# A fused attention-and-MLP kernel: other costs and one more dependency in the projections' planner, and two sums of forms on VectorE

## The chip, the cores and the metric

The kernel runs on one core of one Trainium2 chip. The metric is the device time of one execution in microseconds (us), as the median of several executions. Engine names in the profile: PE is TensorE's matmuls, PEld its weight loads, DVE is VectorE, ACT is ScalarE, POOL is GpSimd, SP is SyncE, which issues DMAs.

## The reference

```
x  = A_x;  xn = layernorm(x)                         # 2048 tokens, 640 channels, fp32
q, k, v = split(xn @ wqkv)                           # 32 heads of 20
pq, pk = q @ w_phi, k @ w_phi                        # per head
phi = concat(softmax(p), softmax(-p))                # of pq and of pk
kv, z = phi_k^T v, sum(phi_k);  o = phi_q kv / (phi_q z + 1e-6)
mlp = gelu(layernorm(xn) @ w1 + b1) @ w2 + b2        # 640 -> 1728 -> 640
out = x + o @ wo + mlp
```

## The kernel before, in words

Every fp32 factor is split into two float32r parts, hi and lo, and a product is three matmuls: hi·hi, hi·lo, lo·hi (`mm3`, L69, L70, L71). A tile's hi part is written by ScalarE as a copy, its lo part by VectorE or GpSimd as a subtraction. PE's order is fixed by the program's text, and so is that of the other three engines from the first stage to the end of the projections. The 2048 tokens are four blocks b of 512, or sixteen tiles t of 128.

**First MLP stage, to about 212 us.** `passes(g, b)` multiplies block b with group g of w1, applies the GELU, and adds the product with w2 to an accumulator; blocks 0 and 1 are done here, with other work put between PE's products by a count of ticks. `next_y` makes block 1's normalized input y[1] channel chunk by chunk: GpSimd centres (L694), VectorE scales (L696), ScalarE copies the hi part (L698), VectorE subtracts the lo part (L700). `turned_forms` (L881 to L900) prepares, for blocks 1 and 0, sums and differences of token halves for a product with seven instead of eight block products ("forms"): two sums hi + lo (L886), four differences (L890), ScalarE's hi copies (L894), two lo parts (L896), and stores to DRAM (`f_dram`).

**Projections, about 212 to 429 us.** Tiles t = 0 to 15 are multiplied with the folded weights wkv for q, k and v (L989, or L1360 and L1364 for pairs of tiles 2 to 7, which use the forms). Each result lies in one of three PSUM banks until ScalarE (L1262, L1001, L1083) and VectorE (L1260, L1088) have read it. `feature_steps` then makes softmax features of k and q: extremes (VectorE, L1011 and L1012), differences (GpSimd, L1021), exponentials (ScalarE, L1024), totals (VectorE, L1029), reciprocals (L1035, L1037), products (GpSimd, L1042 for k, L1044 and L1046 for q), and for k a hi copy (ScalarE, L1051) and a lo part (L1054, on GpSimd or VectorE, whichever the planner takes); for q a transposition (L1063). `kv_tile` (L1102, L1105) multiplies a tile's k features with its v, and L1112 adds part of that up.

The order in this stage comes from `Plan` (L1144 to L1212). Each piece of work is added with an engine, a cost in us and the pieces it comes after. `latest` computes for each piece when it must end at the latest for PE's pieces to run without a wait; `run` then places pieces engine by engine, the most urgent among those that can start, on a clock of these costs. Costs of all engines but PE are multiplied by LONGER (L1214). Pieces of SP count another 4.0 us (LANDS) until their data is there. `plan_sums` (L1426) splits the sums of weight forms into hi (L1438) and lo (L1439). When the four splits of the second half are done, `next_forms(0)` (L1463) issues the load of the first turned forms on SP (`load_forms`, L1141): it goes into the place that held these sums. `plan_pair_splits` (L1500) splits the first w1 weights of the next stage, two halves: hi by ScalarE (L1509), lo by GpSimd (L1510); it returns the two lo pieces as `w1_done`. `plan_second_split` does the first half of w2 (L1521, L1525). At the plan's end stand two PE pieces of 3.4 us that emit nothing (L1559): they stand for the next stage's first products, and came after the release of their PSUM banks alone.

**Second MLP stage, from 429 us,** for blocks 2 and 3, with the attention's last steps beside it; the output projection ends the kernel. Its first products are L69 to L71 with the w1 split by L1509 and L1510: fifteen products of the first half, fifteen of the second; after those thirty the last `kv_tile` (t = 15) is put in (`last_kv`), and then come block 3's thirty and the products with w2, which need block 2's hidden values: gelu (L293), hi (L60), lo (L63).

## Time and profile before

| | |
|---|---|
| median of 3 executions | 708.94 us (707.58 to 709.35) |
| the profiled execution | 707.14 us, with a span of 705.4 us |
| mean granted PE clock | 0.998 |
| PE busy | 693.2 us (98%) |
| VectorE, ScalarE, GpSimd busy | 538.1, 373.2, 503.2 us |

The span runs from the first to the last instruction; 1.7 us of the profiled execution's time lie outside of it. A row of a timeline has the start in us from the span's beginning, the duration, the engine, the line, the operation, what is written <- what is read, and in brackets how long the engine was idle before and what released it. PE's matmuls overlap: two of 512 columns start 0.23 us apart, though each is shown as 0.39 us long.

### The profile page before, as it was taken

To read this page: it belongs to the slowest core of one execution; us is meant where nothing else is said; L and a number is where in the kernel's file an instruction comes from. 1 tells how busy PE (TensorE), PEld (TensorE's weight loads), DVE (VectorE), ACT (ScalarE), POOL (GpSimd) and SP (SyncE) were. 2 spreads that over 40 slices of the span, in tenths; PEclk is the share of its full clock that TensorE was granted. 3 is DMA by queue.
4 is the path that set the end of the run, shared out by engine and by line. 5 is a ranking of instruction groups with operands and counts; after the bars stand their busy time and mean duration, and the time that the engine had idled before them with its cause. 6 is when DMAs were issued, how large, how long until landed. Compare 5 with 4: busy or idle time off the path is not lost.

```text
span 705.4 us, 9865 instructions
## 1 busy us (share of the span) xinstructions
PE 693.2 (98%) x3313; PEld 582.8 (83%) x3313; DVE 538.1 (76%) x884; ACT 373.2 (53%) x633; POOL 503.2 (71%) x373
## 2 busy tenths in 40 slices
PE   9999999999999899999999997999999999999998
PEld 7878888888888788888888886888888888888886
DVE  7888664987767988888678868758678687789783
ACT  6435654444444544545455546547677666659360
POOL 3744783767276769898988889648689997477930
PEclk9999999999999999999999999999999999999999
DMA  9816768575531115464631637774345648881212
GB/s 327 257 48 181 238 178 262 180 259 181 185 120 74 60 61 208 106 198 168 151 110 57 148 114 285 199 228 127 123 133 169 182 148 278 294 280 65 76 74 105
DMA packets 72376, 117.06 MB, mean 166 GB/s; under 512 B 8054, under 2 KB 36502, under 8 KB 70318
## 3 DMA queue, kind: packets, MB, share of 16 engines
q1 hardware_dynamic: 72022, 116.42, 51.3%
q8 instruction: 26, 0.43, 0.3%
q14 instruction: 24, 0.20, 0.1%
q10 hardware_dynamic: 304, 0.01, 0.0%
HBM read 76.62 MB, written 39.79 MB: 165 GB/s over the span
## 4 chain that ended last, share of the span: by engine, by line
PE 88%; DVE 6%; POOL 2%; issue 1%; DMA 1%; ACT 1%; DVEq 0%; SPq 0%; ACTq 0%; POOLq 0%
PE bank L989 19%; PE bank L69 18%; PE bank L71 18%; PE bank L70 18%; PE bank L1360 4%; PE bank L1102 2%; PE bank L650 2%; PE bank L1713 1%; PE bank L1714 1%; POOL m L1021 1%; PE bank L1364 1%; PE bank L556 1%; DVE xb L696 1%; DVE y L700 1%; DMA w<-f 1%
## 5 line engine op out<-in xcount | busy, mean ns | idle before, releaser
L69 PE MATMUL bank<-m,w 128*128 128x512 f32 x288 | 113.0, 392 | 0.0
L70 PE MATMUL bank<-m,w 128*128 128x512 f32 x288 | 112.1, 389 | 0.0
L71 PE MATMUL bank<-m,w 128*128 128x512 f32 x266 | 103.6, 389 | 0.0
L989 PE MATMUL bank<-wkh,y 128*128 128x512 f32 (+1 forms) x360 | 101.0, 355 | 0.0
L70 PE MATMUL bank<-y,w 128*128 128x512 f32 (+1 forms) x256 | 99.4, 388 | 0.8 <-DVE y L700 0.8
L69 PE MATMUL bank<-y,w 128*128 128x512 f32 (+1 forms) x256 | 100.2, 391 | 0.0
L71 PE MATMUL bank<-y,w 128*128 128x512 f32 (+1 forms) x246 | 96.0, 390 | 3.8 <-POOL w L1510 3.8
L63 POOL TENSOR_TENSOR w<-r,w 128x640 fp32r<-128x640 f32 x29 | 48.2, 1676 | 34.9 <-ACT w L60 30.3
L989 PEld LDWEIGHTS bank<-wkh,y 128*128 128x128 f32 x360 | 65.0, 188 | 8.1
L69 PEld LDWEIGHTS bank<-m,w 128*128 128x128 f32 x288 | 54.1, 188 | 11.6 <-DVE acc L338 0.4
L989 PE MATMUL bank<-wkl,y 128*128 128x512 f32 (+1 forms) x180 | 63.7, 354 | 0.0
L70 PEld LDWEIGHTS bank<-m,w 128*128 128x128 f32 x288 | 54.1, 188 | 10.9
L71 PEld LDWEIGHTS bank<-m,w 128*128 128x128 f32 x266 | 49.9, 188 | 10.5
L71 PEld LDWEIGHTS bank<-y,w 128*128 128x128 f32 x246 | 46.6, 189 | 14.1 <-POOL w L1510 4.7
L989 PE MATMUL bank<-w,y 128*128 128x512 f32 x240 | 57.5, 391 | 0.0
L70 PEld LDWEIGHTS bank<-y,w 128*128 128x128 f32 x256 | 48.5, 189 | 10.9 <-DVE y L700 1.3
L69 PEld LDWEIGHTS bank<-y,w 128*128 128x128 f32 x256 | 48.5, 190 | 10.4 <-ACT bank L1781 0.3
L338 DVE TENSOR_TENSOR acc<-bank,acc 128x512 f32<-128x512 f32 x70 | 47.2, 683 | 12.6 <-PE bank L71 6.9
L1029 DVE TENSOR_REDUCE sm<-m 128x64 f32<-128x1280 f32 x32 | 47.1, 1471 | 9.0 <-ACT m L1024 8.6
L1262 ACT ACTIVATE m<-bank 128x512 f32<-128x512 f32 (+2 forms) x48 | 20.8, 468 | 58.7 <-PE bank L989 41.1
L989 PEld LDWEIGHTS bank<-w,y 128*128 128x128 f32 x240 | 44.4, 188 | 8.6
L1707 POOL TENSOR_TENSOR e<-e,m 128x512 fp32r<-128x512 f32 x28 | 40.1, 1435 | 15.7 <-ACT m L1706 14.8
(290 smaller groups left out, 1720.5 us busy)
## 6 DMA issues: line engine op xcount, KB each, us to landing
r<-in_w SPq DMA_DIRECT2D x52, 320.0 KB
e<-e SPq DMA_DIRECT2D x40, 256.0 KB
e<-acc SPq DMA_DIRECT2D x52, 160.0 KB
f<-xq SPq DMA_DIRECT2D x16, 256.0 KB
t<-t SPq DMA_DIRECT2D x8, 512.0 KB
acc<-in_xT SPq DMA_DIRECT2D x3, 1280.0 KB
w<-f SPq DMA_DIRECT2D x3, 1024.0 KB
tf<-t SPq DMA_DIRECT2D x2, 1536.0 KB
```

Of the source, the lines that this page charges most:

```text
L63: eng.tensor_tensor(lo, src, f(hi), op=ALU.subtract)
L69: nc.tensor.matmul(ps, lh, rh, start=first, stop=False, **kw)
L70: nc.tensor.matmul(ps, lh, rl, start=False, stop=False, **kw)
L71: nc.tensor.matmul(ps, ll, rh, start=False, stop=last, **kw)
L338: nc.vector.tensor_tensor(acc[b][:, m, :], pw, acc[b][:, m, :], op=ALU.add)
L650: nc.tensor.matmul(ps[:, u * nh * DF:(u + 1) * nh * DF], raw[:nh * DH, u * P:(u + 1) * P], wpt[:nh * DH, g, :nh, 1:], start=True, stop=True)
L989: nc.tensor.matmul(ps, lh[:, kc, c], rh[:, kc], start=n == 0, stop=n == 3 * KC - 1)
L1029: nc.vector.tensor_reduce(sm, e.rearrange("p a (h f) -> p (a h) f", f=DH), axis=AX, op=ALU.add)
L1102: nc.tensor.matmul(kvp[g // 2][:, (g % 2) * 240:(g % 2) * 240 + 240].rearrange("p (i c) -> p i c", i=2), v[:, g * VS:(g + 1) * VS], ft[:, ...
L1262: nc.scalar.activation(o, src, AF.Copy)
L1360: nc.tensor.matmul(ps, left(yn, pl, q), right(w, pr, q), start=first and q == 0 and n == 0, stop=False, skip_group_check=True)
L1707: mlp.after(1, lambda: nc.gpsimd.tensor_tensor(pl, e, f(ph), op=ALU.subtract))
```

## The change

Four edits. The first two sums of `turned_forms` (for block 1, q = 1) go from GpSimd to VectorE. LONGER goes from 1.05 to 1.02, so every cost that is not PE's counts less. The cost of `next_forms(0)` on SP goes from 0.7 to 3.5 us. The two PE pieces at the plan's end also come after `w1_done`.

```
-                nc.gpsimd.tensor_tensor(o, *(f(z[:, c]) for z in y[b]), op=ALU.add)
+                (nc.vector if b and q else nc.gpsimd).tensor_tensor(o, *(f(z[:, c]) for z in y[b]), op=ALU.add)
...
-    LANDS, SOON, HURRY, AFTER, LONGER = 4.0, 0.9, -1.0, 10.0, 1.05
+    LANDS, SOON, HURRY, AFTER, LONGER = 4.0, 0.9, -1.0, 10.0, 1.02
...
-        w_ready["s1"] = (*w_ready["s1"], plan.add("SP", 0.7, lambda: next_forms(0), *done))
+        w_ready["s1"] = (*w_ready["s1"], plan.add("SP", 3.5, lambda: next_forms(0), *done))
...
-        plan.add("PE", 3.4, lambda: None, *bank_free[(n + i) % 3])
+        plan.add("PE", 3.4, lambda: None, *bank_free[(n + i) % 3], *w1_done)
```

PE's order is the same in both kernels. Three places on the other engines:

**The two sums, in the first MLP stage.** On VectorE before (`m_640`, `m_668`: lo parts of hidden values; `wkl`: lo parts of folded weights):

```order
L741 TENSOR_TENSOR wkl<-bank_548,wkh 128x4x6x19
L63 TENSOR_TENSOR m_640<-bank_641,m_640 128x512
L741 TENSOR_TENSOR wkl<-bank_564,wkh 128x6x19
L741 TENSOR_TENSOR wkl<-bank_564,wkh 128x3x6x19
L63 TENSOR_TENSOR m_668<-bank_669,m_668 128x512
```

and now:

```order
L741 TENSOR_TENSOR wkl<-bank_548,wkh 128x4x6x19
L63 TENSOR_TENSOR m_640<-bank_641,m_640 128x512
L886 TENSOR_TENSOR xq<-y_150,y_151 128x512
L741 TENSOR_TENSOR wkl<-bank_564,wkh 128x6x19
L741 TENSOR_TENSOR wkl<-bank_564,wkh 128x3x6x19
L886 TENSOR_TENSOR xq<-y_150,y_151 128x512
L63 TENSOR_TENSOR m_668<-bank_669,m_668 128x512
```

Each sum now stands between two pieces that read PSUM banks. On GpSimd the two stood right behind the five L694, ahead of the four L890; they are gone from there.

**The load of the turned forms, at the start of the projections.** On VectorE before (L1439: lo parts of the weight sums, `w_2148` the place they come from; L1088: reads of PSUM banks for v; the load follows the L1439 of `s`):

```order
L1011 TENSOR_REDUCE mx<-m_2136 128x32
L1012 TENSOR_REDUCE mx<-m_2136 128x32
L1088 SCALAR_TENSOR_TENSOR v_2129<-bank_2240,rs_all,v_2129 128x10x48
L1088 SCALAR_TENSOR_TENSOR v_2129<-bank_2240,rs_all,v_2129 128x32
L1035 RECIPROCAL w<-sm 128x64
L1439 TENSOR_TENSOR acc_2261<-w_2148,acc_2261 128x512
L1439 TENSOR_TENSOR wkl<-w_2148,wkh 128x512
L1439 TENSOR_TENSOR acc_2261<-w_2148,acc_2261 128x512
L1011 TENSOR_REDUCE mx<-m_2135 128x32
L1012 TENSOR_REDUCE mx<-m_2135 128x32
L1088 SCALAR_TENSOR_TENSOR v_2132<-bank_2297,rs_all,v_2132 128x11x12
L1439 TENSOR_TENSOR s_2262<-w_2148,acc_2261 128x512
```

and now:

```order
L1011 TENSOR_REDUCE mx<-m_2136 128x32
L1012 TENSOR_REDUCE mx<-m_2136 128x32
L1439 TENSOR_TENSOR wkl<-w_2148,wkh 128x512
L1088 SCALAR_TENSOR_TENSOR v_2129<-bank_2241,rs_all,v_2129 128x10x48
L1088 SCALAR_TENSOR_TENSOR v_2129<-bank_2241,rs_all,v_2129 128x32
L1439 TENSOR_TENSOR acc_2261<-w_2148,acc_2261 128x512 x2
L1439 TENSOR_TENSOR s_2262<-w_2148,acc_2261 128x512
L1035 RECIPROCAL w<-sm 128x64
L1011 TENSOR_REDUCE mx<-m_2135 128x32
L1012 TENSOR_REDUCE mx<-m_2135 128x32
L1088 SCALAR_TENSOR_TENSOR v_2132<-bank_2297,rs_all,v_2132 128x11x12
```

All four L1439 stand ahead of the reciprocal, of the second pair of extremes and of one L1088; the load needs the last of them.

**The next stage's weights, at the end of the projections.** On GpSimd before, from the first w1 split on (`w_4063`, in the new kernel `w_3934`: the two halves of w1; `w_4183` and `w_4107`: w2; `m_...`: features):

```order
L1510 TENSOR_TENSOR w_4063<-r_4055,w_4063 128x640
L1042 TENSOR_TENSOR m_4069<-m_4069,w 128x1280
L1021 TENSOR_TENSOR m_4151<-m_2136,mx 128x32x20
L1021 TENSOR_TENSOR m_4151<-mx,m_2136 128x32x20
L1510 TENSOR_TENSOR w_4063<-r_4056,w_4063 128x640
L1630 MEMSET kvs 128x1408
```

and now, from the second w1 split on:

```order
L1510 TENSOR_TENSOR w_3934<-r_3910,w_3934 128x640
L1042 TENSOR_TENSOR m_3993<-m_3993,w 128x1280
L1021 TENSOR_TENSOR m_4080<-m_2135,mx 128x32x20
L1021 TENSOR_TENSOR m_4080<-mx,m_2135 128x32x20
L1021 TENSOR_TENSOR m_4104<-m_2136,mx 128x32x20
L1021 TENSOR_TENSOR m_4104<-mx,m_2136 128x32x20
L1525 TENSOR_TENSOR w_4107<-r_4047,w_4107 128x640
L1042 TENSOR_TENSOR m_4080<-m_4080,w 128x1280
L1021 TENSOR_TENSOR m_4159<-m_2136,mx 128x32x20
L1021 TENSOR_TENSOR m_4159<-mx,m_2136 128x32x20
L63 TENSOR_TENSOR w_4107<-r_4048,w_4107 128x640
L1630 MEMSET kvs 128x1408
```

The second L1510 now stands ahead of the last two L1042 and the last three pairs of L1021, and both w2 splits (L1525, L63) ahead of the memset, where they stood behind it and four short products. ScalarE's L1509 and SP's loads move forward with them. Elsewhere in the projections, three of the sixteen lo parts of k (L1054) go from GpSimd to VectorE: ten of VectorE's instead of seven. On VectorE, behind the last `kv_tile`, the lo part of block 2's first hidden values (L63) now stands behind L1112, a reciprocal, five L1619, L1621, the other half's L63 and four L1063; before, it stood ahead of them.

## The prediction

> **What bounds the kernel now.** I read the page first, then the list of PE's waits, then the timelines around each of them.

> ```profile
> PE 693.2 (98%) x3313; PEld 582.8 (83%) x3313; DVE 538.1 (76%) x884; ACT 373.2 (53%) x633; POOL 503.2 (71%) x373
> ...
> PE bank L71 <- POOL w L1510: 3.8, 1, 3.8
> PE bank L1360 <- DMA w<-f: 2.2, 1, 2.2
> ...
> PE bank L70 <- DVE y L700: 0.8, 1, 0.8
> ```

> PE is busy for 693.2 of 705.4 us. PE's work is the same in both kernels, so the change can only act on PE's waits. Besides one at the program's start three are above 0.2 us (columns: sum, times, longest), and they are what the edits aim at: the second half of w1 (L1510), the turned forms' load, and y[1]'s lo part (L700). The first costs more than its 3.8 us. The windows around it (last columns: granted clock, DMA share, GB/s):

> ```profile
> 240.00:244.00 4.00, 1.82 (x8) 1.24 (x7) 4.00 (x5) 1.14 (x1) 2.50 (x2) 1.00 0.62 242
> 245.00:429.00 184.00, 184.00 (x967) 160.26 (x965) 148.49 (x243) 93.43 (x144) 160.91 (x111) 1.00 0.44 129
> ...
> 433.00:437.00 4.00, 0.43 (x2) 0.00 (x1) 3.66 (x5) 1.75 (x3) 4.00 (x3) 1.00 1.01 409
> 437.00:441.00 4.00, 3.74 (x10) 2.99 (x11) 2.96 (x5) 2.56 (x3) 3.84 (x6) 0.57 0.97 402
> ```

> Behind the 3.8 us the clock falls to 0.57 for a few us; behind the 2.2 us (240:244) it stays at 1.00. And from 245 to 429 us PE has no gap at all: 184.00 of 184.00.

> **The change part by part.** First the two sums. PE, VectorE and GpSimd around 41 to 45 us, and what follows the sums:

> ```profile
> 43.77 0.39 PE L69 MATMUL bank<-y,w 128*128 128x512 f32 x1
> 44.99 0.50 PE L70 MATMUL bank<-y,w 128*128 128x512 f32 x1 [0.84 <-DVE y L700]
> 43.10 1.28 POOL L886 TENSOR_TENSOR xq<-y,y 128x512 f32<-128x512 f32 x1 [1.23 <-DVE y L700]
> 44.34 3.63 POOL L890 TENSOR_TENSOR xq<-xq 128x256 f32<-128x256 f32 x4
> 41.02 1.40 DVE L696 TENSOR_TENSOR xb<-xb,m 128x512 f32<-128x512 f32 x1
> 42.34 0.68 DVE L700 TENSOR_TENSOR y<-xb,y 128x512 fp32r<-128x512 f32 x1
> 43.55 1.39 DVE L700 TENSOR_TENSOR y<-xb,y 128x512 fp32r<-128x512 f32 x1
> 57.32 0.69 DVE L63 TENSOR_TENSOR m<-bank,m 128x512 fp32r<-128x512 f32 x1 [1.37 <-ACT m L60]
> 59.24 1.16 ACT L894 ACTIVATE xq<-xq 128x512 fp32r<-128x512 f32 x2
> 63.95 1.37 ACT L60 ACTIVATE w<-r 128x640 fp32r<-128x640 f32 x2 [3.54 <-PE bank L71]
> ```

> VectorE's subtraction takes 0.68 us alone (42.34). While GpSimd runs its second sum (43.10), the last L700 takes 1.39; the L696 ahead of it, beside the first sum, took 1.40: the two engines hold each other up. Without the sums L700 ends 0.72 + 0.71 = 1.4 us earlier, at 43.5 instead of 44.9. PE wants it 0.23 us behind 43.77, at 44.0, so the whole delay of 44.99 - 44.00 = **1.0 us** goes (0.5 if only the later collision matters). The sums cost VectorE 2 x 0.68 around 55 us, where 1.37 us of idle time cover them. GpSimd's four L890 (3.63 us) now start after the sums and end near 60 us, instead of 48; ScalarE wants them at 59.24, and has 3.54 us to spare behind. So I cost the move at nothing; without that cover it would be about 1 us.

> [...]

> Second, the forms' load, with PE's wait, the load (a row of the chain: issue, us to landing) and VectorE's queue:

> ```profile
> 240.91 0.39 PE L1364 MATMUL bank<-wkh,y 128*128 128x512 f32 x1
> 243.48 0.70 PE L1360 MATMUL bank<-m,w 128*128 128x512 f32 x2 [2.18 <-DMA w<-f]
> 238.57 4.77 DMA w<-f
> 229.10 0.81 DVE L1012 TENSOR_REDUCE mx<-m 128x32 f32<-128x640 f32 x1
> 231.07 1.34 DVE L1439 TENSOR_TENSOR acc<-w,acc 128x512 fp32r<-128x512 f32 x1
> 232.34 2.85 DVE L1439 TENSOR_TENSOR wkl<-w,wkh 128x512 fp32r<-128x512 f32 x1
> 235.11 0.68 DVE L1439 TENSOR_TENSOR acc<-w,acc 128x512 fp32r<-128x512 f32 x1
> 237.43 0.99 DVE L1439 TENSOR_TENSOR s<-w,acc 128x512 fp32r<-128x512 f32 x1
> 241.99 0.68 DVE L1260 TENSOR_TENSOR m<-bank,m 128x512 f32<-128x512 f32 x1
> 250.41 1.29 PE L1102 MATMUL bank<-w,v 128*128 128x240 f32 x10
> ```

> PE starts 2.57 us after the matmul before instead of 0.23: 2.34 us lost. In the new order L1439 begins when L1012 ends, near 229.8, with only the two reads of L1088 between (under 0.9). Four at 0.68 make the load start at 233.4; the four measured (1.34 + 2.85 + 0.68 + 0.99 = 5.9) make it 236.6. I take 234.5, nearer the first, because one of the four (235.11) does take 0.68 and GpSimd's product that could hold the others up, L1042, now waits for a reciprocal behind them. Landing 4.77 us later: 239.3, at worst 241.4. PE wants it at 241.1, so the wait is gone, or 0.3. Late next is L1260, which ended at 242.7 and frees a bank that PE now wants 2.3 us sooner; I put 0.3 us on that (0 to 1.3), so **2.0 us** is gained (1.0 to 2.3). The reciprocal and L1042 slip by about the four splits, 3 to 6 us; the features they lead to are wanted by PE only at 250.4 (the first `kv_tile`), which hides it; uncovered it would be those 3 us.

> Third, the next stage's weights:

> ```profile
> 429.08 0.44 PE L69 MATMUL bank<-y,w 128*128 128x512 f32 x1
> 433.04 0.39 PE L70 MATMUL bank<-y,w 128*128 128x512 f32 x1
> 437.26 0.80 PE L71 MATMUL bank<-y,w 128*128 128x512 f32 x1 [3.83 <-POOL w L1510]
> 440.75 0.39 PE L70 MATMUL bank<-y,w 128*128 128x512 f32 x1
> 434.42 2.79 POOL L1510 TENSOR_TENSOR w<-r,w 128x640 fp32r<-128x640 f32 x1
> 429.62 2.38 POOL L1042 TENSOR_TENSOR m<-m,w 128x1280 f32<-128x1280 f32 x1
> 433.19 1.28 POOL L1021 TENSOR_TENSOR m<-mx,m 128x640 f32<-128x640 f32 x1
> 443.49 1.58 POOL L1525 TENSOR_TENSOR w<-r,w 128x640 fp32r<-128x640 f32 x1 [1.50 <-ACT w L1521]
> 433.34 2.47 DVE L1054 TENSOR_TENSOR w<-m,w 128x1280 fp32r<-128x1280 f32 x1 [0.77 <-ACT w L1051]
> 439.64 0.89 DVE L63 TENSOR_TENSOR m<-m,m 128x512 fp32r<-128x512 f32 x1 [1.01 <-ACT m L60]
> 441.66 1.27 DVE L1063 STREAM_TRANSPOSE acc<-m 128x320 f32<-128x320 f32 x3
> ```

> The delay is 437.26 - 433.04 - 0.23 = 3.99 us; then eight matmuls to 440.75 take 3.49 instead of 8 x 0.23 = 1.82 us at the lowered clock: 1.67 more, **5.66 us** in all. The second L1510 now stands ahead of two L1042, six L1021 and L1525, which by these rows take 2 x 2.38 + 6 x 1.28 + 1.58 = 14.0 us. It ends near 437.2 - 14.0 = 423, ten us before PE wants it. This wait goes for sure, and the low clock with it.

> What is late next? (a) Tile 15's `kv_tile` comes after thirty products, 429.1 + 6.9 = 436.0; its lo part (L1054) ended at 435.8. On GpSimd one L1510 and L1525 more now stand ahead of its L1042: 0 to 1.5 us. (b) After sixty products and the `kv_tile`, at about 429.1 + 13.8 + 1.4 = 444.3, PE wants the lo part of the first hidden values, which was ready at 439.64 + 0.89 = 440.5. Now it follows the `kv_tile` (1.29 long, so its end is about 437.3) by fourteen VectorE pieces, itself the last: four L1063 (1.27 / 3 = 0.42 each) and the eight small ones (L1112, L1037, five L1619, L1621) at as much make 5.0, the two L63 between 0.69 (57.32) and 1.39 each (L700's, held up). So it ends between 443.6 and 445.0, and if the small ones take half as long again, at 447.5. I take 1.5 us for (b) (0 to 3), the middle, since L63 can't begin before ScalarE's copy either, and 0.5 for (a) and whatever else crowds there. Both leave the clock alone, since 2.18 us did. Gain: 5.66 - 2.0 = **3.7 us** (1.2 to 5.7).

> LONGER itself makes no work; its trace in the order is three L1054 that move to VectorE. PE's 184.00 of 184.00 covers that, with seven of them there already.

> Sum: 1.0 + 2.0 + 3.7 = **6.7 us**. Against the profiled execution's own 707.14 us (1.7 outside the span, unchanged) this is 700.4; that execution was 1.8 us below the median of 708.94, so I forecast 702.2 us as a median.

> **The rivals.** (1) *The wait only moves.* If the hidden values of (b) come over 3 us late, the clock falls again, since 3.83 us did that, and the third part gives nothing: 1.0 + 2.0 = 3.0 us, 705.9. For: the L63 stands behind pieces that themselves wait for GpSimd. Against: it needs 3 us over the walk above. [...]

> (2) *The order does not do what it says.* ScalarE's L1509 stands earlier in ScalarE's queue; if its raw weights have not landed, it holds all bank reads behind it. If their load takes as long as that of the forms and is issued only as its turn comes, one hold of 4.77 us eats most of the sum: 702.2 + 4.77 = 707.0, which can't be told from no change. Against: the loads move forward together with their users.

> (3) *VectorE becomes the bound: slower.* VectorE's L1054 and GpSimd's work hold each other, and two of the moved ones now stand ahead of an L1088 that frees a bank:

> ```profile
> 239.80 1.47 DVE L1054 TENSOR_TENSOR w<-m,w 128x1280 fp32r<-128x1280 f32 x1
> ```

> If each of the ten makes PE wait, the change turns slower from 0.67 us each (6.7 / 10); at the hold of 2.47 (the L1054 of 433.34) - 1.47 = 1.00 us it is 702.2 + 10.0 = 712.2. Against: the seven of before left PE no gap between 245 and 429 us.

> **How the numbers follow.** The forecast 0.70, (1) 0.14, (2) 0.10, (3) 0.06. The best case is 1.0 + 2.3 + 5.7 = 9.0 us, 699.9; the least of the forecast's is 0.5 + 1.0 + 1.2 = 2.7 us, 706.2, which takes in (1). The three executions of before lie up to 1.4 us from their median; with half of that or so at either end the range is 699.0 to 706.8. About 0.3% (2.1 us) is what a measurement of this kernel can tell from no change: forecast and (1) are faster by more, 0.84; (2) is the same, 0.10; (3) slower, 0.06.

> **What would show it.** In the changed kernel's profile PE's waits for L1510, for w<-f and for L700 are gone; the load is issued near 234 us; the clock stays at 1.00 from 433 to 441 us; a wait of L70 for DVE m L63 appears near 440 us. PE gaps between 245 and 425 us, or a wait over 3 us behind the first sixty products, would make the prediction wrong.

## The result, and the profile after

| | before | changed | ratio, 95% interval |
|---|---|---|---|
| first set, medians of 5 | 709.03 us | 700.23 us | 0.9871 (0.9855 to 0.9888) |
| second set, medians of 23 and 4 | 708.89 us | 699.31 us | 0.9868 (0.9852 to 0.9884) |
| profiled execution shown | 707.14 us | 699.09 us | |

The change makes the kernel 1.3% faster, 9.4 us by the second ratio; forecast were 6.7 us, and the measured time lies in the range, 0.3 to 1.2 us above its lower end of 699.0. In one execution of the first set the granted clock fell to 0.16 at 244 us and stayed there (2847 us; the ratio leaves it out, the median of 5 has it). The profile shown is of the second set (e1 below), with a span of 697.2 us.

The page's engine row, and the list of PE's waits, as they answer to those of before:

```profile
PE 690.6 (99%) x3313; PEld 581.8 (83%) x3313; DVE 540.1 (77%) x889; ACT 372.5 (53%) x633; POOL 491.8 (71%) x368
```

```profile
PE bank L70 <- DVE m L63: 0.8, 1, 0.8
...
PE bank L69 <- DVE v L1088: 0.4, 1, 0.4
```

The waits for L1510, w<-f and L700 are gone. What is new is what the prediction called (b), L70 waiting for the hidden values' lo part, and 0.4 us for a bank. The windows of the same stages (last columns: granted clock, DMA share, GB/s):

```profile
240.00:244.00 4.00, 4.00 (x19) 3.32 (x18) 3.61 (x6) 2.00 (x2) 2.92 (x3) 1.00 0.00 0
245.00:425.00 180.00, 180.00 (x949) 156.96 (x947) 151.90 (x241) 91.59 (x143) 155.56 (x110) 1.00 0.45 135
425.00:429.00 4.00, 3.61 (x18) 2.92 (x17) 4.00 (x8) 2.30 (x5) 3.14 (x3) 1.00 1.01 368
...
433.00:437.00 4.00, 4.00 (x24) 3.47 (x23) 3.16 (x7) 3.99 (x9) 3.84 (x6) 1.00 0.98 408
437.00:441.00 4.00, 4.00 (x19) 3.08 (x17) 4.00 (x10) 1.58 (x4) 3.23 (x3) 1.00 0.60 205
441.00:445.00 4.00, 3.24 (x15) 2.58 (x15) 4.00 (x8) 2.98 (x6) 3.17 (x5) 1.00 0.60 162
```

PE is full from 245 to 425 us, as it was before, although VectorE is busier there (151.90 of 180, where it was 148.49 of 184). The clock stays at 1.00 throughout. The three places in the timelines, first the sums (VectorE, GpSimd, ScalarE):

```profile
43.07 0.68 DVE L700 TENSOR_TENSOR y<-xb,y 128x512 fp32r<-128x512 f32 x1
53.44 0.68 DVE L886 TENSOR_TENSOR xq<-y,y 128x512 f32<-128x512 f32 x1
55.05 0.68 DVE L886 TENSOR_TENSOR xq<-y,y 128x512 f32<-128x512 f32 x1
54.20 0.75 POOL L890 TENSOR_TENSOR xq<-xq 128x256 f32<-128x256 f32 x1 [16.41 <-DVE xq L886]
55.88 2.35 POOL L890 TENSOR_TENSOR xq<-xq 128x256 f32<-128x256 f32 x3 [0.93 <-DVE xq L886]
58.17 1.16 ACT L894 ACTIVATE xq<-xq 128x512 fp32r<-128x512 f32 x2
62.86 1.37 ACT L60 ACTIVATE w<-r 128x640 fp32r<-128x640 f32 x2 [3.54 <-PE bank L71]
```

The last L700 takes 0.68 us again. The sums cost VectorE 0.68 each; GpSimd's differences end at 58.2 us, where ScalarE takes them up, and ScalarE's 3.54 us to spare are untouched. Then the load (VectorE, SP's queue, and PE's first product with the forms):

```profile
228.15 0.81 DVE L1012 TENSOR_REDUCE mx<-m 128x32 f32<-128x640 f32 x1
228.88 1.35 DVE L1439 TENSOR_TENSOR wkl<-w,wkh 128x512 fp32r<-128x512 f32 x1
...
232.44 0.68 DVE L1439 TENSOR_TENSOR s<-w,acc 128x512 fp32r<-128x512 f32 x1
233.27 0.32 SPq L1141 DMA_DIRECT2D w<-f  x1
239.71 0.84 PE L1360 MATMUL bank<-m,w 128*128 128x512 f32 x3
```

It is issued at 233.27 (238.57 before; the L1012 ahead shows that 0.95 us of this is the earlier gain, 228.15 against 229.10), and PE goes on without a gap. And the next stage's weights (GpSimd, VectorE, PE):

```profile
411.65 1.56 POOL L1510 TENSOR_TENSOR w<-r,w 128x640 fp32r<-128x640 f32 x1
423.93 1.49 DVE L1029 TENSOR_REDUCE sm<-m 128x64 f32<-128x1280 f32 x1 [1.62 <-ACT m L1024]
425.34 0.35 DVE L1088 SCALAR_TENSOR_TENSOR v<-bank,rs_all,v 128x132 fp32r<-128x132 f32 x1
425.74 0.50 PE L69 MATMUL bank<-y,w 128*128 128x512 f32 x1 [0.39 <-DVE v L1088]
430.20 2.27 DVE L1054 TENSOR_TENSOR w<-m,w 128x1280 fp32r<-128x1280 f32 x1
440.74 0.39 PE L69 MATMUL bank<-m,w 128*128 128x512 f32 x1
440.93 0.90 DVE L63 TENSOR_TENSOR m<-m,m 128x512 fp32r<-128x512 f32 x1
441.89 0.50 PE L70 MATMUL bank<-m,w 128*128 128x512 f32 x1 [0.76 <-DVE m L63]
```

The second L1510 begins at 411.65 instead of 434.42 (3.9 us of this are the two earlier gains). L63 ends at 441.8; PE wanted it at 440.74 + 0.23 = 440.97, and with the pace just behind the wait the loss there is 1.0 us.

### The profile page after: what moved, and what is told of

It is laid out like the page before. It is cut to its first block, busy times and chain, and to the rows that moved or that the text cites. A ratio compares the mean times of both kernels' runs of the same rounds, so it can differ in the third digit from the quotient of the medians.

```text
span 2845.1 us, 9865 instructions
## 1 busy us (share of the span) xinstructions
PE 2838.9 (100%) x3313; PEld 2093.5 (74%) x3313; DVE 531.0 (19%) x889; ACT 373.6 (13%) x633; POOL 475.7 (17%) x368
## 4 chain that ended last, share of the span: by engine, by line
PE 99%; DMA 0%; DVE 0%; SPq 0%; ACT 0%; issue 0%
PE bank L989 28%; PE bank L69 18%; PE bank L71 18%; PE bank L70 18%; PE bank L1360 5%; PE bank L1102 4%; PE bank L1713 2%; PE bank L1714 2%; PE bank L1364 1%; PE bank L315 1%; PE bank L333 1%; PE bank L334 1%; PE bank L314 1%; PE bank L650 0%; PE bank L1649 0%; PE bank L1105 0%
## 5 line engine op out<-in xcount | busy, mean ns | idle before, releaser
L989 PE MATMUL bank<-wkh,y 128*128 128x512 f32 (+1 forms) x360 | 411.3, 1291 | 0.0
L989 PEld LDWEIGHTS bank<-wkh,y 128*128 128x128 f32 x360 | 280.9, 795 | 68.1 <-issue 66.5
L69 PE MATMUL bank<-m,w 128*128 128x512 f32 x288 | 319.0, 1108 | 0.0
L70 PE MATMUL bank<-m,w 128*128 128x512 f32 x288 | 317.8, 1103 | 0.0
L989 PE MATMUL bank<-w,y 128*128 128x512 f32 x240 | 290.5, 1522 | 0.0
L71 PE MATMUL bank<-m,w 128*128 128x512 f32 x266 | 281.4, 1058 | 0.0
L69 PE MATMUL bank<-y,w 128*128 128x512 f32 (+1 forms) x256 | 273.9, 1070 | 0.0
L70 PE MATMUL bank<-y,w 128*128 128x512 f32 (+1 forms) x256 | 272.0, 1063 | 0.0
L71 PE MATMUL bank<-y,w 128*128 128x512 f32 (+1 forms) x246 | 253.9, 1032 | 0.0
L989 PEld LDWEIGHTS bank<-w,y 128*128 128x128 f32 x240 | 193.4, 809 | 77.2 <-issue 76.1
L989 PE MATMUL bank<-wkl,y 128*128 128x512 f32 (+1 forms) x180 | 229.9, 1277 | 0.0
L70 PEld LDWEIGHTS bank<-m,w 128*128 128x128 f32 x288 | 169.1, 587 | 68.1 <-issue 63.1
L69 PEld LDWEIGHTS bank<-m,w 128*128 128x128 f32 x288 | 168.8, 586 | 68.3 <-issue 59.8
L71 PEld LDWEIGHTS bank<-m,w 128*128 128x128 f32 x266 | 148.0, 556 | 60.4 <-issue 55.2
L70 PEld LDWEIGHTS bank<-y,w 128*128 128x128 f32 x256 | 147.6, 577 | 56.3 <-issue 51.8
L69 PEld LDWEIGHTS bank<-y,w 128*128 128x128 f32 x256 | 146.8, 573 | 57.1 <-issue 50.7
L71 PEld LDWEIGHTS bank<-y,w 128*128 128x128 f32 x246 | 138.0, 561 | 53.0 <-issue 47.8
L989 PEld LDWEIGHTS bank<-wkl,y 128*128 128x128 f32 x180 | 143.9, 799 | 35.0 <-issue 34.1
L1102 PEld LDWEIGHTS bank<-w,v 128*128 128x128 f32 x160 | 114.5, 931 | 12.1 <-issue 12.1
L1102 PE MATMUL bank<-w,v 128*128 128x240 f32 x160 | 107.8, 1015 | 0.0
```

What stands on the lines that cost most here:

```text
L69: nc.tensor.matmul(ps, lh, rh, start=first, stop=False, **kw)
L70: nc.tensor.matmul(ps, lh, rl, start=False, stop=False, **kw)
L71: nc.tensor.matmul(ps, ll, rh, start=False, stop=last, **kw)
L989: nc.tensor.matmul(ps, lh[:, kc, c], rh[:, kc], start=n == 0, stop=n == 3 * KC - 1)
L1102: nc.tensor.matmul(kvp[g // 2][:, (g % 2) * 240:(g % 2) * 240 + 240].rearrange("p (i c) -> p i c", i=2), v[:, g * VS:(g + 1) * VS], ft[:, ...
```

## The experiments

All medians are given beside before's on the same chip; "us" in the tables is the ratio's distance from 1 times 708.9.

**The four edits, each alone, and the whole.** The whole (e1) has no edit of its own. Recorded for the four runs:

> The changed kernel as it is, for a profile at full clock. Measured so far: 9.1 us below before (0.9871). Theory A (every wait goes with all of it, nothing is late next): PE's waits for L700, w<-f and L1510 are absent, the clock is 1.00 from 433 to 441 us, no wait of L70 for DVE m L63 over 0.3 us near 440; the span is 9.0 us below that of before (1.0 + 2.3 + 5.7). Theory B (the on-record terms of 1.0, 2.0 and 3.7 are right, and something else gives 2.4 us more): a wait of about 1.5 us near 440 is there, and a gain of over 2 us shows at a place that the prediction does not name.

```
 e2: before, with
-                nc.gpsimd.tensor_tensor(o, ...
+                (nc.vector if b and q else nc.gpsimd).tensor_tensor(o, ...
```

> Before with the two sums on VectorE alone; nothing else is changed. Theory A: PE's wait for L700 goes, 1.0 us faster (708.0). Theory B: the collision with GpSimd is only part of it or VectorE's two sums hold up bank reads at 50 to 57 us: 0.5 us faster to 0.5 slower.

```
 e3: before, with
-    plan.add("SP", 0.7, lambda: next_forms(0), *done)
+    plan.add("SP", 3.5, lambda: next_forms(0), *done)
```

> Before with the cost of the forms' load alone at 3.5. Theory A: the wait for w<-f goes with all of it, 2.3 to 2.7 us faster (706.4). Theory B: L1260's bank or the load itself is late next, 1.7 to 2.0 us faster (707.1), with a PE gap of 0.3 us or more at 241 to 244 us.

```
 e4: before, with
-        plan.add("PE", 3.4, lambda: None, *bank_free[(n + i) % 3])
+        plan.add("PE", 3.4, lambda: None, *bank_free[(n + i) % 3], *w1_done)
```

> Before with the extra dependency on the two w1 splits alone. The second L1510 stands ahead of one L1042 and four L1021 here (two and six in the changed kernel): by the rows of before 2.4 + 4 x 1.3 + 1.6 = 9 us earlier, still 5 us ahead of PE. Theory A: wait and low clock go with nothing late next, 5.7 us faster (703.2). Theory B: a wait of 1.5 us near 440 takes their place and 0.5 us are lost to a late kv_tile, 3.7 us faster (705.2).

And LONGER alone, which came with the second group:

```
 e8: before, with
-    LANDS, SOON, HURRY, AFTER, LONGER = 4.0, 0.9, -1.0, 10.0, 1.05
+    LANDS, SOON, HURRY, AFTER, LONGER = 4.0, 0.9, -1.0, 10.0, 1.02
```

> Before with LONGER alone at 1.02. Theory L (it gives room that only the early splits use): the waits for L1510 and w<-f are both there, no wait for L1054 in either, within 0.7 us of before (708.2 to 709.6). Rival (the gain that the single edits leave open, 9.4 less 1.0, 3.6 and 1.6, is LONGER's own): 3 us faster (705.7).

| | median us | ratio (95%) | us |
|---|---|---|---|
| e1 all four | 699.31 | 0.9868 (0.9852 to 0.9884) | -9.4 |
| e2 sums alone | 707.88 | 0.9983 (0.9970 to 0.9996) | -1.2 |
| e3 load's cost alone | 705.24 | 0.9950 (0.9936 to 0.9963) | -3.5 |
| e4 dependency alone | 707.31 | 0.9982 (0.9967 to 0.9997) | -1.3 |
| e8 LONGER alone | 712.72 | 1.0058 (1.0043 to 1.0073) | +4.1 |

Taken alone, the four add up to -1.9 us, not to -9.4. e2 is what both the prediction and theory A said. e3 gives more than the 2.3 to 2.7 us of either theory. e4 and e8 are far off every expectation, and both miss in the same place. PE's waits of e4, and the windows around the second wait for L1054:

```profile
PE bank L1360 <- DMA w<-f: 2.2, 1, 2.2
PE bank L1102 <- DVE w L1054: 1.8, 1, 1.8
PE bank L1102 <- POOL w L1054: 1.4, 1, 1.4
```

```profile
439.24:442.65 3.41, 1.63 (x12) 1.21 (x11) 3.41 (x3) 2.82 (x3) 3.33 (x4) 1.00 0.84 352
442.65:446.07 3.42, 3.42 (x12) 2.84 (x11) 3.31 (x9) 3.41 (x10) 1.87 (x2) 0.50 0.16 44
```

With the dependency alone the wait for L1510 goes, and two waits for the k lo parts of tiles 14 and 15 come in its place, with a fall of the clock to 0.50 behind the second. In e8 PE stands at the third product of the stage, and no longer at the eighteenth as before (PE, then GpSimd's two splits):

```profile
430.36 0.44 PE L69 MATMUL bank<-y,w 128*128 128x512 f32 x1
439.04 0.80 PE L71 MATMUL bank<-y,w 128*128 128x512 f32 x1 [8.02 <-POOL w L1510]
```

```profile
424.50 1.58 POOL L1510 TENSOR_TENSOR w<-r,w 128x640 fp32r<-128x640 f32 x1
...
436.20 2.79 POOL L1510 TENSOR_TENSOR w<-r,w 128x640 fp32r<-128x640 f32 x1
```

The last of them begins about as late as before (434.42 there), but the two have changed places. GpSimd's order of before has the first half of w1 ahead (r_4055), that of e8 the second (r_3998):

```
before: L1510 TENSOR_TENSOR w_4063<-r_4055,w_4063 128x640
        ...
        L1510 TENSOR_TENSOR w_4063<-r_4056,w_4063 128x640
e8:     L1510 TENSOR_TENSOR w_4006<-r_3998,w_4006 128x640
        ...
        L1510 TENSOR_TENSOR w_4006<-r_3997,w_4006 128x640
```

So the half that the stage's third product needs comes last. Neither split has a user in PE's list that would make it urgent, and the planner's own times (worked out from its code and costs, not measured) say what the smaller costs do. At 1.05 the second half's lo part is placed at 218.65, ahead of the last PE piece at 220.28. At 1.02 it comes at 219.55, behind that piece at 219.42. What is placed behind PE's last piece is kept back (`rest` in `run`) and issued after the fixed order has ended (`order.close()`); there this piece moved ahead of the first half's, which itself slipped from 211.03 to 217.40. This is read from the planner and the two orders; no run changes that alone.

**The whole without one edit.** Each is the changed kernel with one line as in before.

> The changed kernel with LONGER back at 1.05; the other three edits stay. With the extra dependency alone PE waited 1.8 and 1.4 us for lo parts of k (L1054) in the last two kv_tiles, with a fall of the clock behind it. Theory L (the smaller LONGER is what makes room for the early splits): these two waits are here too, PE loses 1.6 + 1.9 + 1.4 in place of the 0.5 + 1.0 of the changed kernel, 3.4 us slower than it (702.7). Theory N (LONGER does nothing, as I costed it, and the waits for L1054 belong to the old place of the load): within 0.7 us of the changed kernel (699.3 to 700.0).

> The changed kernel with the cost of the forms' load back at 0.7. PE's wait for w<-f is back: 2.3 us and 0.4 us ahead of it. Theory C (the clock falls behind this wait in some executions and not in others): the executions lie in two groups, mean granted clock 1.000 at about 702.1 and 0.998 at about 703.7. Theory D (the wait costs its length and nothing else): all executions near 702.1 at clock 1.000.

> The changed kernel with the two sums back on GpSimd. Both theories of the total: PE's wait for L700 is back, 1.0 to 1.1 us slower than the changed kernel (700.4). If the sums on VectorE cost something elsewhere (a wait for L63 or L173 at 80 to 95 us), under 0.7 us slower.

> The changed kernel without the extra dependency of the two PE pieces on the w1 splits; the other three edits stay. Theory L (LONGER's 1.02 lets the splits slip later unless that dependency holds them): PE's wait for L1510 is 8.0 us, as with LONGER alone, with a fall of the clock behind it, and the time is that of LONGER alone less the sums' 1.2 and the load's 2.6 to 3.6: 708.4 (707.9 to 708.9). Rival (the slip of 8 us belongs to LONGER with the old place of the load): the wait is 3.8 us as before, 5.7 us above the changed kernel, 705.0.

| the changed kernel without | median us | ratio (95%) | us | so the edit gives, as the last one |
|---|---|---|---|---|
| e5 LONGER | 702.61 | 0.9916 (0.9900 to 0.9932) | -6.0 | 3.4 |
| e6 the load's cost | 701.90 | 0.9905 (0.9889 to 0.9922) | -6.7 | 2.7 |
| e7 the sums on VectorE | 700.65 | 0.9885 (0.9869 to 0.9901) | -8.2 | 1.2 |
| e12 the dependency | 708.50 | 0.9996 (0.9987 to 1.0006) | -0.3 | 9.1 |

e5 is theory L to 0.1 us (702.7). Its two waits are those of e4 (1.8 and 1.4 us for L1054), and its GpSimd (the lo part of tile 14, the split) and VectorE (the lo part of tile 15) say why:

```profile
422.57 2.93 POOL L1054 TENSOR_TENSOR w<-m,w 128x1280 fp32r<-128x1280 f32 x1 [2.16 <-ACT w L1051]
425.45 1.57 POOL L1510 TENSOR_TENSOR w<-r,w 128x640 fp32r<-128x640 f32 x1
...
433.16 2.48 DVE L1054 TENSOR_TENSOR w<-m,w 128x1280 fp32r<-128x1280 f32 x1 [0.36 <-ACT w L1051]
```

At 1.05 tile 14's lo part stays on GpSimd, and the second split comes only behind it and ahead of tile 15's last pieces, which then end too late. At 1.02 tile 14's goes to VectorE, the split is done at 413.2, and tile 15's lo part starts at 430.20, 3 us earlier. How many of the sixteen L1054 an engine has shows that this takes both edits. VectorE has ten of them in the changed kernel, seven with the dependency and 1.05 (e4, e5), as before, and six with 1.02 and no dependency (e8, e12). e8's:

```profile
L1054 POOL TENSOR_TENSOR w<-m,w x10: 2951/2960/2978, 254.3 to 426.0; 128x1280 fp32r<-128x1280 f32 x10
L1054 DVE TENSOR_TENSOR w<-m,w x6: 1472/2298/2705, 240.9 to 435.1; 128x1280 fp32r<-128x1280 f32 x6
```

e12 is theory L as well: the splits are swapped as in e8, its list has L1510 with 8.0 us again, and behind it the clock is at 0.50 from 433 to 437 us. So three of the four edits without the dependency give nothing measurable, and the dependency and LONGER work only together. e7 came out as expected, with the wait for L700 back (0.9 us). In e6 the wait came back in two parts, and theory C's two groups did not appear: all four executions had a clock of 0.999 or 1.000.

```profile
PE bank L1360 <- DVE v L1088: 1.3, 1, 1.3
...
PE bank L1360 <- DMA w<-f: 1.0, 1, 1.0
```

e8 has two such parts too (1.3 and 1.2 us), so at 1.02 the load's old cost gives another order than at 1.05.

**Does the clock fall behind the wait for the load?** e3's 3.5 us were more than the wait that it removed. In the profiled execution of before the clock stayed at 1.00 behind that wait; in that of e2, where wait (2.11 us) and place are the same, it fell to 0.50 (e2's first product behind the wait, then the window around the wait and the one after it):

```profile
243.57 0.94 PE L1360 MATMUL bank<-m,w 128*128 128x512 f32 x3 [2.11 <-DMA w<-f]
```

```profile
241.23:244.65 3.42, 1.31 (x7) 0.93 (x6) 3.39 (x6) 0.08 (x1) 2.50 (x2) 1.00 0.47 196
244.65:248.06 3.41, 3.41 (x10) 2.64 (x9) 1.85 (x3) 1.88 (x2) 3.03 (x3) 0.50 0.00 0
```

e4's profile has the same fall (0.67 from 244 to 246 us, 0.50 from 246 to 248). To see it alone, the changed kernel's load was held up by another load ahead of it, of half the data (e10: `8 * P`) or of all (e11: `16 * P`):

```
+        if t == 2:
+            nc.sync.dma_start(f(place)[:, :8 * P], f_dram[t // 4][t % 4 // 2].rearrange("p q i l n -> p (q i l n)")[:, :8 * P])
         nc.sync.dma_start(f(place), f_dram[t // 4][t % 4 // 2].rearrange("p q i l n -> p (q i l n)"))
```

> The changed kernel with the first load of forms delayed by a load of half the same data into the same place ahead of it, which it must wait for (the result stays the same). PE's wait for w<-f should be back at about 1 to 2 us, here as the only wait of that stage. Theory C (the length of the wait decides whether the clock falls; 2.3 us sits where it does in some executions and not in others): below 2 us no fall, all executions at clock 1.000, slower than the changed kernel by the wait alone (700.5 to 701.5). Rival (a fall needs a second wait a few us before it, as 0.4 us ahead of 2.3, or 1.6 ahead of 1.9): no fall either; the longer delay decides.

> The same with a load of all of the data ahead: PE's wait for w<-f about 3 us, alone. Theory C: the clock falls in most or all executions, mean 0.998, and the time is the wait and about 1.6 us above the changed kernel (704.0); if the wait comes out at 2.3 us, two groups 1.5 us apart. Rival (a second wait is needed): clock 1.000 in all, the wait alone (702.4).

e10 took 701.76 us (0.9901, 0.9885 to 0.9917), e11 705.35 us (0.9946, 0.9930 to 0.9961). PE behind the wait, and the windows around it, of e10:

```profile
242.65 0.94 PE L1362 MATMUL bank<-m,w 128*128 128x512 f32 x3 [1.88 <-DMA w<-f]
```

```profile
239.30:242.71 3.41, 1.53 (x8) 0.98 (x6) 3.34 (x5) 1.56 (x2) 1.98 (x3) 1.00 0.62 252
242.71:246.12 3.41, 3.41 (x15) 2.82 (x16) 1.80 (x3) 1.75 (x2) 2.33 (x2) 1.00 0.00 0
```

And of e11:

```profile
242.84 1.62 PE L1362 MATMUL bank<-m,w 128*128 128x512 f32 x3 [3.16 <-DMA w<-f]
```

```profile
238.62:242.04 3.42, 1.06 (x5) 0.56 (x3) 3.35 (x5) 1.15 (x1) 2.24 (x2) 1.00 0.82 307
242.04:245.45 3.41, 2.61 (x6) 2.15 (x7) 1.38 (x3) 0.00 (x0) 2.32 (x2) 0.50 0.00 0
245.45:248.86 3.41, 3.41 (x9) 2.64 (x8) 0.00 (x0) 1.86 (x2) 1.79 (x3) 0.50 0.00 0
```

Those are the waits of the profiled executions; the others' clocks alone are known. With a lone wait of 1.9 us four of five executions kept a clock of 0.999 to 1.000; the fifth had 0.997 and was the slowest, 703.04 us. With 3.2 us five of six had 0.995 to 0.998; the sixth kept 1.000, at 703.03 us. The rival, that a second wait is needed, falls with e11. Theory C holds in part: more executions fell behind the longer wait, though five and six are few, and the length alone did not decide.

What else differed is in the traces. The windows above are cut at changes of the clock, or at multiples of 3.413 us, called steps here, from a change in the same execution (second column: how long PE is busy). Before's clock was at 0.50 from 437.23 to 440.64 us, for 3.413 us, and its next change, behind the last instruction, is at 706.88, 78 steps on. e2's two falls are 194.6 us apart, 57 steps (its clock is 0.66 from 244 to 246 us and 0.65 from 438 to 442). The low stretches are one step long in before, in e2 and behind the load in e4 (3.4 us), and two in e3, e8, e11 and e12 (6.8 us), at 0.50. Counted from the span's beginning, the changes lie 0.32 us behind a whole number of steps in before, 2.30 in e2 and 3.11 in e11. So a wait can fall into one step, as e2's of 2.11 us, or be shared by two, as before's of 2.18 us in its own steps (PE busy for 2.05 and 2.60 us). And e5's second wait is as long as e4's (1.78 us) and left the clock at 1.00:

```profile
239.25:242.67 3.42, 2.05 (x9) 1.33 (x8) 3.42 (x6) 1.87 (x2) 1.62 (x3) 1.00 0.84 304
242.67:246.08 3.41, 2.60 (x11) 2.17 (x12) 3.34 (x4) 0.89 (x2) 2.48 (x2) 1.00 0.01 2
```

```profile
432.38:435.79 3.41, 1.63 (x8) 1.04 (x6) 3.01 (x4) 2.82 (x4) 3.37 (x4) 1.00 0.95 404
435.79:439.21 3.42, 3.42 (x21) 3.02 (x22) 3.30 (x7) 3.41 (x8) 2.81 (x2) 1.00 0.25 96
```

With PE busy for 1.06 (e11) or 1.31 us (e2) of a step the clock fell at its end; with 1.53 (e10), 1.63 (e5) or 2.05 us (before) it did not. One step does not sort so: behind e4's, with 1.63 us, it fell. Most of its products have 240 columns (L1102) and not 512; whether that is the reason is open.

**The wait that is left.** The lo part of the first hidden values on GpSimd:

```
 e9: the changed kernel, with
-            split(hh, hl, gt)
+            split(hh, hl, gt, eng=nc.gpsimd if out else nc.vector)
```

> The changed kernel with the lo part of block 2's first hidden values (L63) on GpSimd in place of VectorE, where it stands ahead of L401 and leaves VectorE's queue behind the last kv_tile. Theory A (the 0.8 us wait of L70 is VectorE's queue): the wait goes, with about 1.0 us of PE's loss at 441 us; 1.0 us faster than the changed kernel (698.3). Rival (GpSimd's subtraction takes about 1.5 us, starts behind L1046 and runs into VectorE's work): a wait of L70 for POOL m L63 of 0.3 to 1 us is left, less than 0.5 us faster.

```profile
437.86 1.75 POOL L63 TENSOR_TENSOR m<-m,m 128x512 fp32r<-128x512 f32 x1
```

It took 698.44 us, ratio 0.9855 (0.9837 to 0.9873). GpSimd has it done at 439.6, and the wait of L70 is no longer in the list: theory A. It is the fastest of all kernels here, but its interval overlaps that of the changed kernel (0.9868), so that it beats it rests on the profiles: spans of 695.8 and 697.2 us.

## Why the prediction was right, step by step

**The sums, 1.0 us.** Right. L700 fell back to 0.68 us, the wait went, the cover held. Measured 1.2 us alone (e2) and 1.2 as the last edit (e7). VectorE was not held up by GpSimd there: that engine had been idle for 16.41 us when the first sum ended, and both sums took 0.68 us.

**The load, 2.0 us.** Mechanism right, size low. It was issued at 233.27, which is 234.2 on before's time axis (0.95 us later), where the walk had 234.5. The 0.3 us set aside for L1260 did not come, and the 0.42 us ahead of the wait at 237 us went too: 2.34 + 0.42 = 2.76 us, and with the pace behind the wait 2.9. As the last edit it gave 2.7 us (e6), alone 3.5 (e3).

**The weights, 3.7 us.** The sum is right to 0.6 us, the reason half wrong. The wait and the low clock behind it went (5.7), and 1.0 us came back at (b), where 1.5 was put. The 0.5 us for (a) and crowding did come, as a bank read by L1088 behind an L1029 (0.4 us net); tile 15's lo part, the fear in (a), was in time. So 5.7 - 1.0 - 0.4 = 4.3 us, and that is what PE's rows give: it is 3.9 us ahead of before at tile 14's `kv_tile` (423.98 against 427.87) and 8.2 us behind (b) (442.69 against 450.89). The split itself ended at 413.2, where the walk had 423. What failed is the step "LONGER itself makes no work; its trace in the order is three L1054 that move to VectorE", with the whole third part put on the dependency. It also moves the order of the two w1 splits, and that of tile 14's lo part and the second split; and alone it moves one L1054 the other way, to GpSimd (e8). The runs show 1.3 us for the dependency alone, 4.1 us lost by LONGER alone, 3.4 us gained by it as the last edit. The total came out because the order of the whole change was priced, in which both are; of the dependency and of LONGER, taken singly, that text would have given a false forecast.

**From the profiled execution to the median.** The profiles' own times differ by 707.14 - 699.09 = 8.05 us (by PE's rows 1.0 + 2.9 + 4.3 = 8.2, the difference of the spans); the sum of 6.7 is 1.3 us short of that. The median came out 702.2 - 699.3 = 2.9 us below the forecast, and the other 1.6 are the step "that execution was 1.8 us below the median", which was carried over to the changed kernel. There the profiled execution lies 0.2 us below the median of its set. The 1.8 us were the clock. One step of 3.41 us at 0.50 takes 0.0024 off the mean of such a span, so 0.998, 0.995 and 0.992 stand, by that estimate, for one, two and three steps: of the 23 executions of before in that set, 8 have a mean granted clock of 0.998 and a mean of 707.6 us, 11 have 0.994 or 0.995 and 709.2 us, 4 have 0.992 and 710.4 us. All four of the changed kernel have 1.000. The profiled execution of before (0.998) was one with a single step, and the median has two; the change removes these too. Which of the two waits they stood behind can't be told for each, since e3, without the wait for the load, had 0.995 in three of five; in its profile the clock stayed low for two steps behind L1510.

**The rivals.** (1), the wait only moves, did not happen to the whole, but it is just what the dependency does alone (e4), at the place of (a) rather than (b). "Both leave the clock alone, since 2.18 us did" was no safe reading of one execution: in e4 it fell behind 1.8 us, the second of two waits. (2) No engine was held: the first L1510 waited 1.0 us for L1509, and PE for neither. (3) Ten L1054 on VectorE made PE wait nowhere between 245 and 425 us.

## What to carry to other kernels

Where a planner sets the order, a cost factor and a missing dependency can't be priced one by one: undo each in the full change, and do each alone, before a gain is put down to one of them. A piece whose user lies beyond the plan's end needs a stand-in that falls due, or its place, and even which of two such pieces comes first, hangs on small costs. A wait of TensorE as long as those here (the shortest behind which the clock fell was e4's of 1.78 us, the longest behind which it did not in a profile was before's of 2.18) should be priced with the fall of the clock as a chance, read from the clocks of many executions and not from the one that was profiled: before's 23 executions, all with the same order, had means from 0.992 to 0.998.
